# Twelve of sixteen token tiles turned by DMA in 16-bit halves, not by TensorE

## The chip, the cores and the metric

The kernel runs on one core of a Trainium2 chip. A core has a matrix engine (PE, TensorE) and three engines for elementwise work: DVE (VectorE), ACT (ScalarE) and POOL (GpSimd). SP (SyncE) does no arithmetic here; it issues DMAs, and the 16 DMA engines of the core carry them out. Every engine runs its own list of instructions in order and waits on semaphores for the others. The metric is the device time of one execution in microseconds (us), the median over runs. A measurement of this kernel can tell about 0.5%, 4.3 us, from no change.

## The reference

The input x is 2048 tokens of 512 values. It is normalized once, and two blocks read the normalized tokens: a linear attention with a learned feature map, and a mixture of eight experts of which each token takes two.

```python
# x [1, 2048, 512]; 32 heads of 16; 8 experts, hidden width 1792
xn = (x - mean(x)) / sqrt(var(x) + 1e-5)
# A: linear attention
q, k, v = split(xn @ wqkv)                        # heads of 16
pq, pk  = q @ w_phi, k @ w_phi                    # per head
phi_q   = concat(softmax(pq), softmax(-pq))       # per head, 32 wide
phi_k   = concat(softmax(pk), softmax(-pk))
kv, z   = phi_k^T @ v, sum_s phi_k                # per head, over all tokens
A       = concat_heads(phi_q @ kv / (phi_q . z + 1e-6)) @ wo
# B: experts
g       = softmax(xn @ wg); top two, renormalized
B       = sum over the two: g_e * gelu(xn @ w1[e]) @ w2[e]
out     = x + A + B
```

## The kernel before

The tokens come in 16 tiles of 128 (a tile: 128 partitions, one token each, 512 values of 4 bytes), in four chunks of four. The names below are the functions of the kernel, with lines of the kernel before.

**What happens to a tile.** `load_x` brings it in. `stats` (L302, L303, DVE), `rstds` (L306 on ACT, L307 on DVE) and `norm` (L313, DVE) normalize it into a slot of SBUF, and `norm` also has SP store it to DRAM, to `xn_rows` (L315), from where tokens are gathered by expert later. The matrix products need the tile turned, with the 512 features on the partitions. `turn` does that: four transpositions of 128x128 on PE (L326) into one bank of PSUM (two banks for tiles 0 to 3). `transp` then makes two copies from there: ACT casts the turned tile to the matrix format into `xTh` (L341, two instructions of 256 columns), and DVE writes what the cast lost into `xTl` (L342, two subtractions that wait for those casts). High and low parts of data and weights are multiplied in three products (L174 to L176; L474 to L476 in `proj_q`).

**What is done with it.** `proj_k(t)` makes the transformed keys of tile t and its gate logits; ACT takes them out of PSUM (L429, L430). The softmax of the keys works on pairs of tiles: `k_sub` (DVE, L439 to L442), `k_exp` (ACT, L449, behind a table load), `k_norm` (DVE, L454 to L456). `proj_v(t)` makes the values (ACT takes them out, L361), `proj_q` the transformed queries (L479). `kv(p)` (PE, L501) sums the products of keys and values of pair p. After `k_norm(7)` and the last logits the routing begins on DVE (L535 onward): it ranks the tokens with a small product on PE (`route_rank`, L575), and orders the slots of the experts. The experts' layers take the rest of the span.

**What sets the order.** The calls stand in one list, written out by hand; each engine takes its instructions in the order of that list. SP and PE are scheduled by hand as well. So an instruction that waits holds back everything behind it on its engine. Buffers come from two pools of slots, and a slot that is freed is given to a later tile; which one is decided when the program is built.

**Around the change.** The list runs, in the part that matters:

- tiles 4 to 7: `norm(4..7)`, `k_sub(0)`, `proj_v(0)`, `proj_v(1)`, `k_sub(1)`, `proj_v(2)`, `proj_v(3)`, then `transp(4..7)` with the turns, `stats(8..11)`, `proj_v(4)`, `proj_v(5)`, `rstds`, `norm(8..11)`;
- tiles 8 to 11: `k_exp(0, 1)`, `k_sub(2)`, `proj_v(6)`, `k_sub(3)`, loads of x for tiles 12 to 15, `proj_v(7)`, `k_norm(0)`, `proj_k(4)`, `k_exp(2, 3)`, `proj_k(5)`, `k_norm(1)`, `transp(8..11)`;
- tiles 12 to 15: `norm(12..15)`, `k_sub(6)`, `proj_k(8)`, `kv(2)`, `kv(3)`, `proj_k(9..11)`, `proj_q(0, 3)`, `transp(12..15)`, `k_norm(5)`, `k_sub(7)`, `k_exp(6, 7)`, `k_norm(6)`, `proj_k(12..14)`, `kv(4)`, `kv(5)`, `proj_k(15)`, `k_norm(7)`, then the routing.

Of the kernel before, what the change touches and what calls it, by code (L numbers as in the profile page):

```python
# [11 lines left out]
F16 = mybir.dt.float16  # L12
I32 = mybir.dt.int32
AF = mybir.ActivationFunctionType
ALU = mybir.AluOpType
# [24 lines left out]
def kernel(  # L40
# [11 lines left out]
    nc = tc.nc  # L52
    P = 128
    S, D = x.shape[1], x.shape[2]
# [256 lines left out]
    def norm(t):  # L311
        n = slot([P, D], name="xn")
        nc.vector.tensor_scalar(n, xt[t // 2][:, t % 2, :], mv[:, t, 0:1], rstd[:, t:t + 1],  # L313
                                op0=ALU.subtract, op1=ALU.mult)
        nc.sync.dma_start(xs[t * 512:(t + 1) * 512, :].rearrange("(p a) f -> p (a f)", a=4), n)  # L315
        xn[t] = n
        if t % 2:
            free(xt.pop(t // 2))

    turned = {}  # L320

    def turn(t):
        a = bank("pT")
        turned[t] = a, bank("pT") if t < 4 else a
        for k in range(KD):
            nc.tensor.transpose(turned[t][k // 2][:, k * P:(k + 1) * P], xn[t][:, k * P:(k + 1) * P], ident)  # L326
        free(xn.pop(t))

    def transp(t):
        c, j = divmod(t, TPC)  # L330
        if j == 0:
            xTh[c] = [slot([P, 2, 512], F32R, name="xTh", keep=c == 1) for _ in range(2)]
            xTl[c] = [slot([P, 2, 512], F32R, name="xTl", keep=c == 1) for _ in range(2)]
        if t not in turned:
            turn(t)
        ps = turned.pop(t)
        for h in range(2):
# [4 lines left out]
            nc.vector.tensor_sub(dl, src, f32(dh))  # L342
        free(*ps[:2 if t < 4 else 1])

# [102 lines left out]
    def k_exp(*ts):  # L447
        for t in ts:
            nc.scalar.activation(ek[t], ek[t], AF.Exp)  # L449
# [404 lines left out]
    k_sub(0)  # L854
    proj_v(0)
    proj_v(1)
    k_sub(1)
    proj_v(2)
    proj_v(3)
    for t in range(4, 8):  # L860
        transp(t)
    for t in range(8, 12):
        stats(t)
    proj_v(4)
    proj_v(5)
# [4 lines left out]
    k_sub(2)  # L870
    proj_v(6)
    k_sub(3)
    for t in range(12, 16):
        load_x(t)
    proj_v(7)
    k_norm(0)
    proj_k(4)
    k_exp(2, 3)
    proj_k(5)
    k_norm(1)  # L880
    for t in range(8, 12):
        transp(t)
    k_norm(2)
    proj_k(6)
    k_norm(3)
    k_sub(4)
# [10 lines left out]
    for t in range(12, 16):  # L897
        norm(t)
    k_sub(6)
    proj_k(8)  # L900
# [5 lines left out]
    proj_q(0, 3)  # L906
    for t in range(12, 16):
        transp(t)
    k_norm(5)
# [803 lines left out]
```

## Time and profile before

| | |
|---|---|
| time, median of three runs | 858.99 us (858.55 to 862.88) |
| the profiled execution | 858.56 us |
| its span in the trace | 856.8 us |
| PE busy | 851.3 us, 99% of the span |
| DVE busy | 663.9 us, 77% |
| ACT busy | 438.7 us, 51% |
| granted clock of PE | 1.000 |

The span is what the trace covers; the execution's own time is 1.8 us longer. "Busy" of an engine counts its instructions, without register work and without the issuing of DMAs. A busy PE need not be at its peak: matmuls overlap in the records, so a row's duration is longer than its distance to the next row, and this distance is what a stream of them costs. In a timeline a row is: start, duration, engine, line, operation, output<-input, and behind the count in brackets how long the engine had been idle and what ended that.

### The profile page before, as it was taken

The numbers are of one execution on the slowest core, as the hardware profiler recorded it, in microseconds if no ns is written. First come the engines' busy times: TensorE is split into PE (matmuls) and PEld (weight loads), VectorE is DVE, ScalarE is ACT, GpSimd is POOL, SyncE is SP. The second block draws the span as 40 slices with busy tenths as digits, with TensorE's granted clock in tenths as the row PEclk, the third lists the DMA queues.
The fourth block names the chain that finished last, engine by engine and source line by source line (L and its number), as shares of the span: only waits on it lengthen the run. The fifth ranks groups of instructions, "written<-read, shape, count | busy, mean of one in ns | idle before, by whom it ended". The sixth has DMA issues, their size and how long they took to land.

```text
span 856.8 us, 15997 instructions
## 1 busy us (share of the span) xinstructions
PE 851.3 (99%) x5889; PEld 767.9 (90%) x5889; DVE 663.9 (77%) x1098; ACT 438.7 (51%) x721; POOL 184.4 (22%) x251
## 2 busy tenths in 40 slices
PE   9999999999999999999999999999999999999998
PEld 8888888899999999999999999998787888888886
DVE  6889899887783478878887877987798989846952
ACT  4453522743834364566456665465675566434541
POOL 5000002010004112511241142115511522340011
PEclk9999999999999999999999999999999999999999
DMA  8220106573317441843364346533752736539733
GB/s 298 99 99 2 50 8 191 167 231 101 123 50 221 143 133 37 253 133 113 97 200 151 111 138 159 176 110 123 229 178 87 232 115 205 175 135 384 258 115 100
DMA packets 123575, 126.99 MB, mean 148 GB/s; under 512 B 12518, under 2 KB 87782, under 8 KB 123488
## 3 DMA queue, kind: packets, MB, share of 16 engines
q1 hardware_dynamic: 115408, 106.10, 38.6%
q0 software_dynamic: 7264, 19.36, 7.0%
q8 instruction: 48, 0.79, 0.4%
q10 hardware_dynamic: 816, 0.43, 0.2%
q14 instruction: 39, 0.32, 0.1%
HBM read 98.62 MB, written 27.25 MB: 147 GB/s over the span
## 4 chain that ended last, share of the span: by engine, by line
PE 99%; DMA 0%; DVE 0%; issue 0%
PE pH L174 12%; PE pH L175 12%; PE pH L176 12%; PE pY L1296 9%; PE pY L1334 6%; PE pY L1335 6%; PE pY L1340 6%; PE pY L1266 4%; PE pY L1336 2%; PE pY L1337 2%; PE pY L1342 2%; PE pV L174 2%; PE pK L174 2%; PE pQ L474 2%; PE pV L176 2%; PE pO L176 2%
## 5 line engine op out<-in xcount | busy, mean ns | idle before, releaser
L1220 ACT ACTIVATE gl<-pH 128x276 f32<-128x276 f32 (+6 forms) x182 | 78.1, 436 | 252.6 <-PE pH L176 237.4
L1225 DVE TENSOR_TENSOR h<-gl,h 128x480 fp32r<-128x480 f32 (+6 forms) x112 | 77.8, 695 | 96.5 <-ACT h L1222 76.8
L1233 POOL DMA_INDIRECT y_rows<-keptN,pidx x83 | 90.6, 1091 | 253.3 <-ACT gl L1220 210.1
L176 PE MATMUL pH<-keptR,ws 128*128 128x258 f32 (+3 forms) x276 | 82.8, 300 | 0.0
L174 PE MATMUL pH<-keptR,ws 128*128 128x270 f32 (+3 forms) x240 | 72.5, 302 | 0.0
L175 PE MATMUL pH<-keptR,ws 128*128 128x270 f32 (+3 forms) x240 | 72.4, 301 | 0.0
L1222 ACT CAST h<-gl 128x480 fp32r<-128x480 f32 (+6 forms) x112 | 70.1, 626 | 3.6
L175 PE MATMUL pH<-xgl,ws 128*128 128x260 f32 (+3 forms) x204 | 64.6, 317 | 0.0
L174 PE MATMUL pH<-xgh,ws 128*128 128x260 f32 (+3 forms) x204 | 64.6, 317 | 0.0
L1335 PE MATMUL pY<-h,ws 128*128 128x388 f32 (+4 forms) x180 | 62.4, 347 | 0.0
L276 ACT CAST ws<-keptN 128x1024 fp32r<-128x1024 f32 x55 | 57.5, 1046 | 6.9 <-PE pY L1266 6.9
L176 PE MATMUL pH<-xgh,ws 128*128 128x272 f32 (+3 forms) x188 | 59.2, 315 | 0.0
L276 ACT CAST keptR<-keptN 128x1024 fp32r<-128x1024 f32 (+4 forms) x75 | 50.6, 705 | 16.4 <-remote 4.4
L1334 PE MATMUL pY<-h,ws 128*128 128x416 f32 (+4 forms) x168 | 58.5, 348 | 0.0
L1296 PE MATMUL pY<-h,ws 128*128 128x480 f32 x228 | 56.3, 381 | 0.0
L971 POOL DMA_INDIRECT keptN<-xn_rows,tidx x30 | 34.3, 1145 | 97.0 <-DVE vv L675 46.9
L279 DVE TENSOR_TENSOR ws<-keptN,ws 128x1024 fp32r<-128x1024 f32 x36 | 43.6, 1211 | 13.9 <-ACT ws L276 13.6
L176 PEld LDWEIGHTS pH<-keptR,ws 128*128 128x128 f32 x276 | 52.1, 189 | 1.3
L1296 PEld LDWEIGHTS pY<-h,ws 128*128 128x128 f32 x228 | 42.3, 188 | 10.8 <-issue 2.9
L175 PEld LDWEIGHTS pH<-keptR,ws 128*128 128x128 f32 x240 | 45.3, 189 | 2.2
L176 PE MATMUL pH<-xgh,keptR 128*128 128x272 f32 (+3 forms) x148 | 47.1, 318 | 0.0
L174 PEld LDWEIGHTS pH<-keptR,ws 128*128 128x128 f32 x240 | 45.1, 188 | 1.2
(339 smaller groups left out, 2397.1 us busy)
## 6 DMA issues: line engine op xcount, KB each, us to landing
keptN<-in_B_w_dram SPq DMA_DIRECT2D x172, 256.0 KB
wr<-in_B_w_dram SPq DMA_DIRECT2D x52, 256.0 KB
keptN<-y_rows SPq DMA_DIRECT2D x16, 512.0 KB
x_slots<-keptN SPq DMA_DIRECT2D x25, 256.0 KB
keptN<-in_A_x_dram SPq DMA_DIRECT2D x16, 256.0 KB
xn_rows<-keptN SPq DMA_DIRECT2D x16, 256.0 KB
keptN<-x_slots SPq DMA_DIRECT2D x32, 128.0 KB
keptN<-in_A_x_dram SPq DMA_DIRECT2D x8, 512.0 KB
```

The source lines that it names most:

```text
L174: nc.tensor.matmul(ps, lh, rh, start=(i == 0), stop=False)
L175: nc.tensor.matmul(ps, lh, rl, start=False, stop=False)
L176: nc.tensor.matmul(ps, ll, rh, start=False, stop=(i == n - 1))
L276: nc.scalar.copy(dst_h, src)
L1220: step[:] = [nc.scalar.activation(g[:, c:c + m], ps[:, :m], AF.Gelu_apprx_tanh)]
L1222: nc.scalar.copy(h[:, 0:full], g)
L1225: nc.vector.tensor_sub(h[:, xw:], g, f32(h[:, 0:full]))
L1233: i = nc.gpsimd.indirect_dma_start(out=to, out_offset=bass.IndirectOffsetOnAxis(ap=rows, axis=0), in_=y, in_offset=None)
L1296: nc.tensor.matmul(ps[i][:, 0:w], ws[z][:, D + i * P:D + i * P + P], h[:, low * xw:low * xw + w], start=st and k == 0, stop=last and k == ...
L1334: nc.tensor.matmul(ps[i][:, 0:w - P], vh, h[:, P:w], start=st, stop=False, skip_group_check=True)
L1335: nc.tensor.matmul(ps[i][:, 0:m], vl, h[:, P:cap], start=False, stop=False, skip_group_check=True)
L1340: nc.tensor.matmul(ps[i][:, 0:m], v[0][:, i * P:(i + 1) * P], h[:, gw + P:], start=False, stop=sp_, skip_group_check=True)
```

## The change

Tiles 0 to 3 are turned as before. For tiles 4 to 15 the four transpositions on PE are gone, and so is the bank of PSUM. In their place:

- `norm` allocates a slot of twice the size; the normalized tile lies in its first half.
- `to_planes(t)`: ACT copies the tile, read as 1024 half-words of 16 bits for each token, into the second half of the slot, sorted into a plane of the 512 low halves and a plane of the 512 high halves (L327 of the changed kernel). Then SP issues one transposing DMA (L331) that turns the 128x1024 half-words, as eight blocks of 128x128, into a slot `pl` that two tiles share.
- `to_words(t)`: ACT joins the turned planes to words of 32 bits again, into the second half of the tile's slot (L336).
- `transp(t)` reads that half in SBUF where it read PSUM before; its two casts and two subtractions stay (now L361, L362).

Lines of other functions move by up to 40: `proj_v`'s L361 is now L381, L429 is L449, L449 is L469, L479 is L499, L315 is L317.

The list of calls is also written anew around these steps: tiles 4 to 7 are turned between `proj_v(0)` and `proj_v(4)`, one at a time, and `stats(8..11)` stand behind `proj_v(4)` and `transp(7)`; for tiles 8 to 11 the planes are made around `proj_v(6)` and `proj_v(7)`, the loads of x for tiles 12 to 15 stand behind them on SP, and the joining stands behind `proj_k(5)` and `proj_k(6)`; for tiles 12 to 15 the planes are made right behind each `norm`, and the joining stands where `transp` stood.

The tile numbers in the names below are those of slots (`keptN_77`) and of banks (`pK_1014`). Two places show what moved.

**ACT, from the reciprocal deviations of tiles 12 to 15 on.** Before: the eight rows behind `rstd` take the keys of tiles 8 to 11 and their logits out of PSUM, then comes one bank of queries, then the casts of the turned tile 12.

```order
L306 ACTIVATE rstd<-mv,epst 128x4 [waits DVE_49]
L429 COPY keptN_82<-pK_1022 128x32x15 [waits DMAHW1_49,DVE_49,PE_49]
L430 COPY logits<-pK_1022 128x8
L429 COPY keptN_82<-pK_1102 128x32x15 [waits DMAHW2_49,DVE_49,PE_49]
L430 COPY logits<-pK_1102 128x8
L429 COPY keptN_72<-pK_1117 128x32x15 [waits DMAHW3_49,DVE_49,PE_49]
L430 COPY logits<-pK_1117 128x8
L429 COPY keptN_72<-pK_1133 128x32x15 [waits DMAHW4_49,DVE_49,PE_49]
L430 COPY logits<-pK_1133 128x8
L479 COPY keptN_77<-pQ_1148 128x512 [waits PE_49]
L341 CAST xTh_1162<-pT_1166 128x2x128 [waits PE_49]
L341 CAST xTh_1163<-pT_1166 128x2x128 [waits DVE_49]
```

Now: four rows that split tiles 12 to 15 stand ahead of the same eight (of which the first three are shown here).

```order
L307 ACTIVATE rstd<-mv,epst 128x4 [waits DVE_49]
L327 COPY keptN_77<-keptN_77 128x1024 [waits DVE_49]
L327 COPY keptN_73<-keptN_73 128x1024 [waits DVE_49,Pool_49]
L327 COPY keptN_75<-keptN_75 128x1024 [waits DVE_49,PE_49]
L327 COPY keptN_74<-keptN_74 128x1024 [waits DMAHW2_49,DVE_49]
L449 COPY keptN_90<-pK_1014 128x32x15 [waits PE_49]
L450 COPY logits<-pK_1014 128x8
L449 COPY keptN_90<-pK_1094 128x32x15 [waits PE_49]
```

Behind the rest of the eight comes, for each tile, a row that joins it, which waits for the transposing DMA, and the two casts:

```order
L499 COPY keptN_80<-pQ_1140 128x512 [waits PE_49]
L336 COPY keptN_77<-keptN_84 128x2x512 [waits DMAHW6_49,Activation_49]
L361 CAST xTh_1155<-keptN_77 128x2x128 [waits Activation_49]
L361 CAST xTh_1156<-keptN_77 128x2x128
L336 COPY keptN_73<-keptN_84 128x2x512 [waits DMAHW0_49]
L361 CAST xTh_1155<-keptN_73 128x2x128 [waits Activation_49]
```

So the first cast of tile 12 now stands behind five more rows of ACT, four splits and a join, and each later tile's casts behind one more.

**SP, from the stores of tiles 4 to 7 on.** Before, the eight stores of tiles 4 to 11 stand together:

```order
L315 DMA xn_rows<-keptN_84 128x512 [waits DMAHW1_49,DVE_49]
L315 DMA xn_rows<-keptN_82 128x512 [waits DMAHW2_49,DVE_49]
L315 DMA xn_rows<-keptN_72 128x512 [waits DMAHW3_49,DVE_49]
L315 DMA xn_rows<-keptN_74 128x512 [waits DMAHW4_49,DVE_49]
L315 DMA xn_rows<-keptN_81 128x512 [waits DMAHW5_49,DVE_49]
L315 DMA xn_rows<-keptN_77 128x512 [waits DMAHW6_49,DVE_49]
```

Now the four transpositions of tiles 4 to 7 stand behind their stores, each waiting for the split of its tile on ACT, and the stores of tiles 8 to 11 behind those:

```order
L317 DMA xn_rows<-keptN_84 128x512 [waits DMAHW1_49,DVE_49]
L317 DMA xn_rows<-keptN_82 128x512 [waits DMAHW2_49,DVE_49]
L317 DMA xn_rows<-keptN_72 128x512 [waits DMAHW3_49,DVE_49]
L317 DMA xn_rows<-keptN_74 128x512 [waits DMAHW4_49,DVE_49]
L331 DMA_TRANSPOSE keptN_76<-keptN_84 128x8x128 [waits DMAHW5_49,PE_49,Activation_49]
L331 DMA_TRANSPOSE keptN_76<-keptN_82 128x8x128 [waits DMAHW6_49,PE_49,Activation_49]
L331 DMA_TRANSPOSE keptN_77<-keptN_72 128x8x128 [waits DMAHW7_49,Activation_49]
L331 DMA_TRANSPOSE keptN_77<-keptN_74 128x8x128 [waits DMAHW0_49,Activation_49]
L317 DMA xn_rows<-keptN_78 128x512 [waits DMAHW1_49,DVE_49]
```

The stores have not moved against each other; the transpositions are between them.

The diff:

```diff
--- before.py
+++ after.py
@@ -11,6 +11,7 @@
 F32R = mybir.dt.float32r
 F16 = mybir.dt.float16
 I32 = mybir.dt.int32
+U16 = mybir.dt.uint16
 AF = mybir.ActivationFunctionType
 ALU = mybir.AluOpType
 AX = mybir.AxisListType
@@ -309,21 +310,40 @@
     xn = {}
 
     def norm(t):
-        n = slot([P, D], name="xn")
+        both = slot([P, 2, D], name="xn")
+        n = both[:, 0, :]
         nc.vector.tensor_scalar(n, xt[t // 2][:, t % 2, :], mv[:, t, 0:1], rstd[:, t:t + 1],
                                 op0=ALU.subtract, op1=ALU.mult)
         nc.sync.dma_start(xs[t * 512:(t + 1) * 512, :].rearrange("(p a) f -> p (a f)", a=4), n)
-        xn[t] = n
+        xn[t] = both
         if t % 2:
             free(xt.pop(t // 2))
 
+    planes = {}
+
+    def to_planes(t):
+
+        a = xn[t].bitcast(U16)
+        nc.scalar.copy(a[:, 1, :].rearrange("p (h c) -> p h c", h=2),
+                       a[:, 0, :].rearrange("p (c h) -> p h c", h=2))
+        if t % 2 == 0:
+            planes[t // 2] = slot([P, 2, D], name="pl")
+        nc.sync.dma_start_transpose(
+            planes[t // 2].bitcast(U16)[:, t % 2, :].rearrange("p (b n) -> p b n", n=P), a[:, 1, :])
+
+    def to_words(t):
+
+        nc.scalar.copy(xn[t].bitcast(U16)[:, 1, :].rearrange("p (x h) -> p h x", h=2),
+                       planes[t // 2].bitcast(U16)[:, t % 2, :].rearrange("p (h x) -> p h x", h=2))
+        if t % 2:
+            free(planes.pop(t // 2))
+
     turned = {}
 
     def turn(t):
-        a = bank("pT")
-        turned[t] = a, bank("pT") if t < 4 else a
+        turned[t] = bank("pT"), bank("pT")
         for k in range(KD):
-            nc.tensor.transpose(turned[t][k // 2][:, k * P:(k + 1) * P], xn[t][:, k * P:(k + 1) * P], ident)
+            nc.tensor.transpose(turned[t][k // 2][:, k * P:(k + 1) * P], xn[t][:, 0, k * P:(k + 1) * P], ident)
         free(xn.pop(t))
 
     def transp(t):
@@ -331,16 +351,16 @@
         if j == 0:
             xTh[c] = [slot([P, 2, 512], F32R, name="xTh", keep=c == 1) for _ in range(2)]
             xTl[c] = [slot([P, 2, 512], F32R, name="xTl", keep=c == 1) for _ in range(2)]
-        if t not in turned:
+        if t < 4 and t not in turned:
             turn(t)
-        ps = turned.pop(t)
+        ps = turned.pop(t) if t < 4 else [xn[t][:, 1, :]] * 2
         for h in range(2):
             dh = xTh[c][h][:, :, j * P:(j + 1) * P]
             dl = xTl[c][h][:, :, j * P:(j + 1) * P]
             src = ps[h][:, h * 256:(h + 1) * 256].rearrange("p (k n) -> p k n", k=2)
             nc.scalar.copy(dh, src)
             nc.vector.tensor_sub(dl, src, f32(dh))
-        free(*ps[:2 if t < 4 else 1])
+        free(*(ps if t < 4 else [xn.pop(t)]))
 
 
     vt = {}
@@ -853,15 +873,25 @@
         norm(t)
     k_sub(0)
     proj_v(0)
+    to_planes(4)
+    to_planes(5)
     proj_v(1)
     k_sub(1)
+    to_planes(6)
+    to_words(4)
+    transp(4)
     proj_v(2)
+    to_planes(7)
+    to_words(5)
+    transp(5)
     proj_v(3)
-    for t in range(4, 8):
-        transp(t)
+    to_words(6)
+    transp(6)
+    proj_v(4)
+    to_words(7)
+    transp(7)
     for t in range(8, 12):
         stats(t)
-    proj_v(4)
     proj_v(5)
     rstds(8, TPC)
     for t in range(8, 12):
@@ -869,19 +899,27 @@
     k_exp(0, 1)
     k_sub(2)
     proj_v(6)
+    to_planes(8)
+    to_planes(9)
     k_sub(3)
+    proj_v(7)
+    to_planes(10)
+    to_planes(11)
     for t in range(12, 16):
         load_x(t)
-    proj_v(7)
     k_norm(0)
     proj_k(4)
     k_exp(2, 3)
+    k_norm(1)
     proj_k(5)
-    k_norm(1)
-    for t in range(8, 12):
+    for t in (8, 9):
+        to_words(t)
         transp(t)
     k_norm(2)
     proj_k(6)
+    for t in (10, 11):
+        to_words(t)
+        transp(t)
     k_norm(3)
     k_sub(4)
     proj_k(7)
@@ -896,6 +934,7 @@
     ln_stats(12)
     for t in range(12, 16):
         norm(t)
+        to_planes(t)
     k_sub(6)
     proj_k(8)
     kv(2)
@@ -905,6 +944,7 @@
     proj_k(11)
     proj_q(0, 3)
     for t in range(12, 16):
+        to_words(t)
         transp(t)
     k_norm(5)
     k_sub(7)
```

## The prediction

> **What bounds the kernel now.** I read the page first: the busy times, then the chain of waits that ended last.
>
> ```profile
> span 856.8 us, 15997 instructions
> PE 851.3 (99%) x5889; PEld 767.9 (90%) x5889; DVE 663.9 (77%) x1098; ACT 438.7 (51%) x721; POOL 184.4 (22%) x251
> PE 99%; DMA 0%; DVE 0%; issue 0%
> ```
>
> PE is busy all the time and is 99% of the chain, so work taken from PE looks like time saved. The change takes 48 transpositions from it. What a group of 16 costs is its distance to the next row, in the PE timeline:
>
> ```profile
> 90.00 1.91 PE L326 MATMUL pT<-ident,keptN 128*128 128x128 f32 x16
> 91.66 0.47 PE L174 MATMUL pK<-wfh,xTh 128*128 128x496 f32 x1
> ```
>
> 1.66 us, and the first product behind it lasts 0.47 us where its neighbours last 0.39, so about 1.74. There are three such groups: 5.2 us is the most that the change can bring, 0.6%.
>
> Next I asked who else is full in the stage where the tiles are turned. Busy times in two stretches of 20 us (PE, PEld, DVE, ACT, POOL, granted clock, DMA share, GB/s):
>
> ```profile
> 80.00:100.00 20.00, 20.00 (x113) 16.71 (x115) 16.01 (x32) 8.98 (x21) 0.97 (x3) 1.00 0.14 53
> 100.00:120.00 20.00, 20.00 (x334) 16.44 (x330) 18.08 (x58) 6.22 (x15) 0.00 (x0) 1.00 0.01 3
> ```
>
> DVE has 18 of 20 us behind 100 us. Its timeline and PE's show that the two finish side by side:
>
> ```profile
> 95.88 1.21 DVE L454 TENSOR_REDUCE sk<-keptN 128x64 f32<-128x1024 f32 x1
> 106.05 1.22 DVE L456 TENSOR_TENSOR keptN<-keptN,sk 128x1024 f32<-128x1024 f32 x1
> 113.30 1.00 DVE L563 TENSOR_TENSOR cum<-cum 128x128 f16<-128x128 f16 x4
> ...
> 99.88 1.27 PE L501 MATMUL kv<-keptN,keptN 128*18 128x32 f32 x128
> 106.69 1.46 PE L501 MATMUL kv<-keptN,keptN 128*18 128x32 f32 x128
> 114.33 0.23 PE L575 MATMUL pR<-m,tri 128*128 128x128 f16 x1
> ```
>
> The last `k_norm` ends at 107.27; the group of `kv` that needs it (pairs 6 and 7) takes 1.46 us where the one at 99.88 takes 1.27, so it already waits there. `cum` ends at 114.30 and PE ranks at 114.33. From 95.88 to 107.27 DVE has no row with an idle time. So PE cannot be earlier there unless DVE is: **the saved 5.2 us become waiting, and what DVE does at 95.88 decides.** What sets that is the turning of tiles 12 to 15, where DVE waits for ACT's casts.
>
> **The change, part by part.** Prices: a copy of 128x1024 on ACT has a near row in the page; those of ACT around tiles 12 to 15 are in its timeline.
>
> ```profile
> L276 ACT CAST ws<-keptN 128x1024 fp32r<-128x1024 f32 x55 | 57.5, 1046 | 6.9 <-PE pY L1266 6.9
> 85.82 0.56 ACT L429 COPY keptN<-pK 128x480 f32<-128x480 f32 x1 [0.87 <-DVE keptN L313]
> 86.33 0.58 ACT L429 COPY keptN<-pK 128x480 f32<-128x480 f32 x1
> 90.19 0.59 ACT L479 COPY keptN<-pQ 128x512 f32<-128x512 f32 x1 [2.12 <-PE pQ L476]
> 90.67 0.38 ACT L341 CAST xTh<-pT 128x256 fp32r<-128x256 f32 x1
> 91.54 0.65 ACT L341 CAST xTh<-pT 128x256 fp32r<-128x256 f32 x2 [0.49 <-DVE xTl L342]
> ```
>
> A split or a join handles 1024 half-words in each partition: 1.05 us if the count of elements decides, as in the first row, and 0.55 if their bytes do. I take 1.05, since the row has the same count; on ACT the next instruction starts about 0.1 before the end of the one before (90.19 + 0.59 against 90.67), so 0.94 in a row of them. The planes are read with a stride of two half-words, which no row shows; at worst that doubles a copy, 2.1 us.
>
> The transposing DMA has no row. Its bounds come from the nearest transfers:
>
> ```profile
> q1 hardware_dynamic: 115408, 106.10, 38.6%
> 35.00:37.00 2.00, 2.00 (x10) 1.68 (x9) 2.00 (x5) 0.60 (x1) 0.00 (x0) 1.00 1.05 402
> 33.82 1.79 SPq L315 DMA_DIRECT2D xn_rows<-keptN  x4
> 149.28 0.53 SPq L979 DMA_DIRECT2D x_slots<-keptN  x1
> 151.70 0.69 DVE L441 TENSOR_TENSOR keptN<-keptN,mk 128x512 f32<-128x512 f32 x1 [0.82 <-DMA x_slots<-keptN]
> ```
>
> Four stores run at 402 GB/s, so 256 KB take 0.65 us of the queues: the lower bound. The queue q1 spends 0.386 x 16 x 856.8 us on 115,408 packets, 46 ns each, of 919 bytes on average. The transposition has 1024 rows of 256 bytes, 64 for each of the 16 engines: 0.8 us if time goes by bytes, 2.9 if each row costs a packet. I take 1.4, nearer the bytes since the store moves as much. From issue to use a store takes 2.4 us (149.28 to 151.70). The Trainium skill is at odds with itself here. "Advanced Engine Details and Errata" (X-Bar Transpose (TRN2)) has transposing DMAs nearly as fast as plain ones, 350 to 400 GB/s, about 0.7 us for a tile. "VectorE: DVE Perf Modes" (The three transpose paths) gives 1309 ns for one block of 128x128, against 390 ns on TensorE, and advises TensorE where PSUM will do; eight blocks one after the other would be 10.5 us. No run has shown either yet.
>
> *Tiles 4 to 7.* DVE before:
>
> ```profile
> 39.26 0.69 DVE L442 TENSOR_TENSOR keptN<-mk,keptN 128x512 f32<-128x512 f32 x1
> 41.54 0.43 DVE L342 TENSOR_TENSOR keptR<-pT,keptR 128x256 fp32r<-128x256 f32 x1 [1.60 <-ACT keptR L341]
> 46.33 0.68 DVE L302 BATCH_NORM_STATS2 st<-keptN 128x6 f32<-128x512 f32 x1
> 62.83 0.42 DVE L342 TENSOR_TENSOR xTl<-pT,xTh 128x256 fp32r<-128x256 f32 x1
> 67.62 1.21 DVE L454 TENSOR_REDUCE sk<-keptN 128x64 f32<-128x1024 f32 x1
> ```
>
> The fourth store is issued about 35.1 and has moved by 37.5. The first transposition follows it (+1.4, and 0.4 to be seen): 39.3. SP issues four of them, at 0.45 each by the stores' row, beside that. Then ACT sets the pace, with a join (0.94), two casts (0.27 each), the eviction of a value bank (0.48), 2.0 a tile, and the split of tile 7 (0.94) once: 39.3 + 8.9 + 0.4 for the last subtraction, 48.5. The statistics of tile 8 began at 46.33: **+2.1**.
>
> *Tiles 8 to 11.* The eight subtractions stand from 62.83 to 67.62, 4.8 us, as each second one waits for a cast behind the bank that it shares. Now nothing is shared, ACT has time ahead (the joins stand behind `proj_k(5)`), and eight in a row cost 2.8: **-2.0**. So DVE is at `norm(12)` as before, 85.3 for 85.19.
>
> *Tiles 12 to 15.* Here the splits go ahead of everything on ACT.
>
> ```profile
> 85.19 1.92 DVE L313 TENSOR_SCALAR keptN<-keptN,mv,rstd 128x512 f32<-128x512 f32 x4
> 88.81 0.69 DVE L442 TENSOR_TENSOR keptN<-mk,keptN 128x512 f32<-128x512 f32 x1
> 91.08 0.42 DVE L342 TENSOR_TENSOR xTl<-pT,xTh 128x256 fp32r<-128x256 f32 x1 [1.59 <-ACT xTh L341]
> 91.95 0.76 DVE L342 TENSOR_TENSOR xTl<-pT,xTh 128x256 fp32r<-128x256 f32 x2 [0.44 <-ACT xTh L341]
> 93.15 0.76 DVE L342 TENSOR_TENSOR xTl<-pT,xTh 128x256 fp32r<-128x256 f32 x2 [0.44 <-ACT xTh L341]
> 95.54 0.42 DVE L342 TENSOR_TENSOR xTl<-pT,xTh 128x256 fp32r<-128x256 f32 x1 [0.44 <-ACT xTh L341]
> ```
>
> The first norm ends near 85.8; four splits to 89.65; the four evictions of keys queued behind them at 0.51 (85.82 to 86.33) and that of the queries (0.48) to 92.2; join and cast to 93.65. The four transpositions land beside that, the last near 92. Before, the first subtraction stood at 91.08. A tile then takes ACT 1.62 (a join of 1.05, which its first cast waits for, and the casts), where it took 1.20 (91.95 to 93.15): the last subtraction ends at 93.65 + 3 x 1.62 + 0.7 = 99.2, and `k_norm(5)` starts there instead of 95.88: **+3.3**. DVE has no idle time up to 107.27 to take it up, so `kv(7)`, the ranking and the start of the experts move by 3.3.
>
> PE in this stage: with two groups of transpositions gone it is through `proj_q(0, 3)` at 90.00 - 3.5 = 86.5 and then waits for tile 12 until 93.65, 7 us with no work. What that does to its clock no row in mid-kernel shows; the start does:
>
> ```profile
> 3.79 1.94 PE L378 MATMUL pF<-ident,keptN 128*128 128x128 f32 x8 [0.19 <-DMA keptN<-in_A_wqkv_dram]
> 8.62 1.04 PE L378 MATMUL pF<-ident,keptN 128*128 128x128 f32 x8
> ```
>
> The same eight transpositions take 1.94 us after the idle start and 1.04 five us later: half the rate for some 6 us. Half rate for 3.4 to 6.8 us (up to as long as it was idle) costs 1.7 to 3.4 us of products. PE then has 15 us to `kv(7)` (91.66 to 106.69) and reaches it at 110.4 to 112.1; DVE at 107.27 + 3.3 = 110.6. So 0 to 1.5 of it shows; I take **+0.6**. A rule of the Trainium skill speaks against the change here ("TensorE: Matmul & The Clock Gate", Part 1: the HAM clock gate): an idle window of about 3.4 us halves the clock, and it comes back after as long a busy one. By it the loss is 1.7 us, the lower end, and the sum would come to +3.3; the start agrees with the halving.
>
> Costed at nothing: the twelve DMAs' traffic (share 0.14 and 0.01 in the stretches above, so it has room) and SP's queue (the loads of x behind `proj_v(7)` are needed at 81 us only). If that cover went, `stats(12)` would be late next.
>
> **Sum:** the first two stages cancel to +0.1, which the +3.3 of the third holds already (it starts from 85.3). Against the profiled execution of 858.56: 858.56 + 3.3 + 0.6 = **862.5**. The median is 858.99, 0.43 above the execution the sum starts from.
>
> **Rivals.**
>
> *The transposition is slow.* Up to about 1.9 us it hides behind ACT's pace of 2.0 a tile; beyond, the joins wait for it, and behind a waiting join on ACT stand the evictions of values and keys and so PE; all twelve then run one behind another ahead of work that waits, and each further us costs 12. At 2.9 (a packet for each row): 858.6 + 12 = 870.5; at 3.5, 878. For: rows of 256 bytes, a quarter of the mean packet. Against: by bytes it is 0.8, well under the threshold. A slow 16-bit copy does the same with less: of the 24 copies about 14 are on the path, so 1.3 us instead of 1.05 gives +3.5 more, 866. If the page with 1309 ns per block is right (eight in series), 12 x 8.6 = 103 us would come on top, 962; that outcome lies inside this rival's chance.
>
> *The clock stays low longer*, as at the start and beyond `kv(7)`: 15 us at half rate cost 7.5, of which 1.9 are covered: +3.3 + 3.0 to 5.6, 865 to 867.
>
> *Copies go by bytes*, 0.55 us: stage 12 to 15 gains 8 x 0.5 = 4.0 against +3.3, tiles 4 to 7 lose nothing: DVE is 2 to 2.7 us earlier and PE follows: 856. Against: the row of 1046 ns.
>
> *DVE's delay is taken up*, somewhere in the routing by waits on DMAs: 859. Against: the tie at 114.33, and 99% of the chain on PE.
>
> **How the numbers follow.** Forecast, 860.5 to 865: 0.50; slow transposition or copies, 866 to 880 and beyond: 0.25; long low clock: 0.10; copies by bytes, 854 to 858: 0.08; taken up: 0.07. The likeliest gives 862.5. The bounds of the unknown prices (0.65 to 2.9 us) give +2.5 to +12, so the range is 859.5 to 872; about 0.1 is left on each side. A measurement tells 0.5%, 4.3 us, from no change: faster is below 854.7, half of the copies' case and a little, 0.05; slower is above 863.3: the slow cases (0.25 + 0.10) and a quarter to a third of the forecast, 0.49; within, 0.46.
>
> **What would show it.** In the changed profile: ACT rows of 128x1024 at 1.05 us; the first transposition seen by ACT near 39.3; DVE's `stats(8)` at 48.5, `norm(12)` at 85.3, `k_norm(5)` at 99.2; a wait of PE of about 7 us ahead of `proj_k(12)`, with 128x496 rows of 0.4 turning to 0.6 and more behind it; `kv(7)` ending near 111.5. Wrong it is if the joins wait long for DMAs (the first rival), or if `k_norm(5)` is at 96 or earlier (the third).

## The result, and the profile after

The change makes the kernel slower: 870.62 us (868.61 to 871.54, four runs) against 860.08 (858.55 to 862.88, four runs), a ratio of 1.0116 with a 95% interval of 1.0081 to 1.015. A second set of runs on another occasion gave 867.54 against 858.06, 1.011 (1.0094 to 1.0125). The profiled execution took 871.54 us, its span is 869.4.

The page of the changed kernel, its head, the chain of waits and the hardware DMA queue:

```profile
span 869.4 us, 15942 instructions
PE 851.6 (98%) x5841; PEld 764.6 (88%) x5841; DVE 663.7 (76%) x1098; ACT 464.3 (53%) x745; POOL 183.4 (21%) x251
PE 90%; ACT 5%; DVE 3%; DMA 1%; issue 1%; SPq 0%; ACTq 0%; DVEq 0%
q1 hardware_dynamic: 128080, 109.24, 40.0%
```

PE was 99% of the chain, now it is 90%. ACT has 25.6 us more work and holds 5% of the chain, DVE 3%. PE lost 48 transpositions, 5.2 us by the prediction's rows, and is busy for as long as before (in the second traces of both kernels 849.2 and 850.6 us). About 2.7 us of what it got back are the clock, as the stretches show (columns as before, the clock ahead of the last two):

```profile
80.00:100.00 20.00, 11.44 (x46) 9.15 (x45) 13.33 (x27) 13.95 (x24) 0.42 (x2) 0.81 0.41 105
100.00:120.00 20.00, 20.00 (x328) 16.42 (x327) 16.83 (x32) 10.02 (x20) 0.22 (x1) 0.93 0.01 3
```

From 80 to 100 us PE works 11.44 of 20 us, at a granted clock of 0.81. Its timeline there, and at the two places where PE and DVE had been level before:

```profile
96.89 0.78 PE L175 MATMUL pK<-wfh,xTh 128*128 128x496 f32 x1 [8.56 <-ACT xTh L361]
97.47 0.61 PE L176 MATMUL pK<-wfl,xTh 128*128 128x496 f32 x1
97.88 0.61 PE L177 MATMUL pK<-wfh,xTl 128*128 128x496 f32 x1
...
103.22 0.39 PE L176 MATMUL pK<-wfl,xTh 128*128 128x496 f32 x1
...
114.66 1.32 PE L521 MATMUL kv<-keptN,keptN 128*18 128x32 f32 x128
122.17 0.23 PE L595 MATMUL pR<-m,tri 128*128 128x128 f16 x1
```

PE waits 8.56 us for ACT's cast of tile 12, then its products stand 0.41 us apart where they stood 0.22 apart, until about 102.7. The ranking is at 122.17 instead of 114.33. DVE, at the statistics of tile 8, the norms of tile 12, the first and the last subtraction of tiles 12 to 15, and `k_norm(5)` and `k_norm(7)`:

```profile
49.92 0.69 DVE L303 BATCH_NORM_STATS2 st<-keptN 128x6 f32<-128x512 f32 x1
...
68.29 0.76 DVE L362 TENSOR_TENSOR xTl<-keptN,xTh 128x256 fp32r<-128x256 f32 x2 [1.18 <-ACT xTh L361]
...
88.12 1.92 DVE L315 TENSOR_SCALAR keptN<-keptN,mv,rstd 128x512 f32<-128x512 f32 x4
...
96.87 0.76 DVE L362 TENSOR_TENSOR xTl<-keptN,xTh 128x256 fp32r<-128x256 f32 x2 [4.45 <-ACT xTh L361]
98.86 0.76 DVE L362 TENSOR_TENSOR xTl<-keptN,xTh 128x256 fp32r<-128x256 f32 x2 [1.22 <-ACT xTh L361]
...
102.84 0.76 DVE L362 TENSOR_TENSOR xTl<-keptN,xTh 128x256 fp32r<-128x256 f32 x2 [1.23 <-ACT xTh L361]
103.51 1.22 DVE L474 TENSOR_REDUCE sk<-keptN 128x64 f32<-128x1024 f32 x1
...
113.70 1.22 DVE L476 TENSOR_TENSOR keptN<-keptN,sk 128x1024 f32<-128x1024 f32 x1
```

`k_norm(5)` starts at 103.51, 7.6 us later than before (95.88), and `k_norm(7)` ends at 114.92 instead of 107.27: the same 7.65. So both engines come to `kv(7)` late by nearly the same. What makes DVE wait is ACT (its groups from 30 to 110 us of the span, then its timeline):

```profile
L336 ACT COPY keptN<-keptN 128x1024 uint16<-128x1024 uint16 x12 | 16.3, 1360 | 1.8 <-DMA keptN<-keptN 1.8
L327 ACT COPY keptN<-keptN 128x1024 uint16<-128x1024 uint16 x12 | 12.0, 1045 | 1.2 <-DVE keptN L315 1.2
L361 ACT CAST xTh<-keptN 128x256 fp32r<-128x256 f32 x16 | 5.7, 405 | 0.3
```

```profile
39.02 1.36 ACT L336 COPY keptN<-keptN 128x1024 uint16<-128x1024 uint16 x1 [1.79 <-DMA keptN<-keptN]
...
88.70 3.89 ACT L327 COPY keptN<-keptN 128x1024 uint16<-128x1024 uint16 x4 [0.83 <-DVE keptN L315]
92.49 0.55 ACT L449 COPY keptN<-pK 128x480 f32<-128x480 f32 x1
...
95.00 1.40 ACT L336 COPY keptN<-keptN 128x1024 uint16<-128x1024 uint16 x1
96.44 0.71 ACT L361 CAST xTh<-keptN 128x256 fp32r<-128x256 f32 x2
97.05 1.34 ACT L336 COPY keptN<-keptN 128x1024 uint16<-128x1024 uint16 x1
```

A split takes 1.045 us, a join 1.36. Twelve joins waited for a transposition only once, 1.79 us at 39.02. In the last stage ACT goes without a pause from the first split at 88.70 to the last cast, and each tile costs it 1.99 us.

**How the runs are compared below.** The start of `norm(4)` on DVE lay at 32.4 to 33.8 us in the twelve further traces and the two above, whatever the kernel. The rest from the ranking to the end of the span was 742.2 to 744.9 us in all of them but the first trace of the change, where it was 747.2. This scatter is as large as some of what is asked for. So three places are given in us after the start of `norm(4)`: the start of `norm(12)`, the end of `k_norm(7)`, the start of the ranking; they repeat within 0.3 us. (`k_sub`, `k_exp`, `k_norm` and `kv` work on one tile each; where the description of the kernel says pair, it should say tile.) One execution of the kernel before, in the set with the median of 858.00 below, took 1709.06 us, and the ratios leave it out. Before: 51.94, 74.02, 81.08. The change: 54.91, 81.71, 88.96.

### The profile page after: what moved, and what is told of

Same layout as the page of the kernel before. It is cut to its first block, busy times and chain, and to the rows that moved or that the text cites. A ratio compares the mean times of both kernels' runs of the same rounds, so it can differ in the third digit from the quotient of the medians.

```text
span 869.4 us, 15942 instructions
## 1 busy us (share of the span) xinstructions
PE 851.6 (98%) x5841; PEld 764.6 (88%) x5841; DVE 663.7 (76%) x1098; ACT 464.3 (53%) x745; POOL 183.4 (21%) x251
## 4 chain that ended last, share of the span: by engine, by line
PE 90%; ACT 5%; DVE 3%; DMA 1%; issue 1%; SPq 0%; ACTq 0%; DVEq 0%
PE pH L175 12%; PE pH L176 12%; PE pH L177 12%; PE pY L1336 8%; PE pY L1374 6%; PE pY L1375 6%; PE pY L1380 6%; PE pY L1306 4%; PE pY L1376 2%; PE pY L1377 2%; PE pY L1382 2%; PE pO L177 1%; PE pO L175 1%; PE pO L176 1%; ACT keptN L336 1%; PE pQ L494 1%
## 5 line engine op out<-in xcount | busy, mean ns | idle before, releaser
L1336 PEld LDWEIGHTS pY<-h,ws 128*128 128x128 f32 x228 | 42.3, 188 | 10.5 <-issue 2.5
```

The source lines that it names most:

```text
L1336: nc.tensor.matmul(ps[i][:, 0:w], ws[z][:, D + i * P:D + i * P + P], h[:, low * xw:low * xw + w], start=st and k == 0, stop=last and k == ...
```

## The experiments

| kernel | norm(12) | k_norm(7) ends | ranking | PE's wait for tile 12 | median us, against before beside it | ratio |
|---|---|---|---|---|---|---|
| before | 51.94 | 74.02 | 81.08 | none | | |
| before, second trace | 51.95 | 74.04 | 81.11 | none | 859.56, one run | |
| the change | 54.91 | 81.71 | 88.96 | 8.56 | 870.62 / 860.08 | 1.0116 (1.0081 to 1.015) |
| the change, second trace | 54.86 | 81.66 | 89.20 | 8.56 | 867.54 / 858.06 | 1.011 (1.0094 to 1.0125) |
| 12 to 15 by PE | 54.91 | 75.30 | 82.38 | 0.98 | 861.34 / 860.77 | 1.0005 (0.9992 to 1.0019) |
| only 8 to 11 by DMA | 51.25 | 72.17 | 79.23 | none | 858.56 / 860.77 | 0.997 (0.9955 to 0.9985) |
| only 12 to 15 by DMA | 51.95 | 78.76 | 85.81 | 3.74 | 862.57 / 858.00 | 1.006 (1.0042 to 1.0078) |
| idle products in the wait | 54.90 | 81.72 | 88.79 | 0.67 | 866.04 / 860.77 | 1.0073 (1.0046 to 1.01) |
| DVE filled | 54.91 | 78.36 | 88.21 | 8.55 | 866.80 / 860.77 | 1.009 (1.0054 to 1.0126) |
| both of these | 54.81 | 78.32 | 86.20 | 0.66 | 863.70 / 858.06 | 1.0065 (1.005 to 1.008) |
| all by DMA, reordered | 51.58 | 75.12 | 82.73 | 3.62 | 860.89 / 858.06 | 1.0034 (1.0022 to 1.0046) |
| join in the other order | 53.58 | 79.68 | 86.76 | 7.92 | 865.22 / 858.00 | 1.0093 (1.0075 to 1.0111) |
| 4 to 11 by DMA, statistics between | 51.53 | 71.94 | 79.01 | none | 856.23 / 858.06 | 0.9978 (0.9968 to 0.9987) |
| that, with the join's other order | 50.21 | 71.31 | 78.36 | none | 855.54 / 858.09 | 0.9971 (0.996 to 0.9981) |

My theory was that two chains end side by side at the ranking: DVE behind ACT's copies, and PE behind its wait and the half rate. The rivals were each of the two alone, and the transposing DMAs.

### Each stage by itself

Tiles 12 to 15 turned by PE, 4 to 11 as in the change:

```diff
-        norm(t)
-        to_planes(t)
+        norm(t)            # t = 12..15
...
-        to_words(t)
         transp(t)          # t = 12..15, with turn(t) on PE
```

> Tiles 12 to 15 turned by PE again, tiles 4 to 11 as in the change. My theory (two chains end side by side at the ranking: DVE behind ACT's copies, PE behind its wait and the half rate): the last stage costs nothing any more, and what is left is the delay that norm(12) already has in the change (88.12 against 85.19). DVE's k_norm(7) ends near 110.2 instead of 107.27 and 114.92, the ranking stands near 117.2 (114.33 before, 122.17 in the change), and the time is about 2.9 us above the kernel before. Rival, the low clock alone makes the loss: with no wait of 8 us left the time is that of the kernel before or up to 3 us below it. Rival, the transposing DMAs make the loss: 8 of 12 are left, and so about two thirds of it, 7 us.

The ranking is 1.3 us later than before, where I expected 2.9; the time is that of the kernel before within 0.2%. So 6.6 of the 7.9 us go when the last stage is taken back. Of the 2.97 us by which `norm(12)` is late, 1.7 come back in the last stage, since PE, with two groups of turns less to do, stands ready for tile 12 where DVE had waited 1.59 us before.

Only tiles 8 to 11 by DMA (the order of the kernel before for 4 to 7 and 12 to 15):

> Only tiles 8 to 11 by DMA; tiles 4 to 7 and 12 to 15 turned by PE in the order of the kernel before. My theory: this stage gives DVE 0.6 to 2 us (the subtractions no longer share a bank with the casts) and PE 1.7, so the ranking comes 0.6 to 1.7 us earlier than 114.33 and the time is 0.6 to 1.7 us below the kernel before. Rival, every transposing DMA and its copies cost time wherever they stand: a third of the loss, +2.5 to +3.5 us.

It is 0.3% faster, with an interval that leaves out 1, though the gain is below the 0.5% that a measurement of this kernel can tell by itself: `norm(12)` comes 0.69 us earlier, and the ranking 1.85, a little more than I expected. That two thirds of it appear only in the last stage has the reason just given. Eight of the twelve DMAs were to cost about 7 us by the third rival and four of them about 3; the ranking moved by +1.3 and by -1.85. The third rival falls here.

Only tiles 12 to 15 by DMA:

> Only tiles 12 to 15 by DMA, with the lines of the change in that stage; tiles 4 to 11 turned by PE in the order of the kernel before. Measured by differences in the change, this stage alone makes DVE 4.7 us later, and tiles 4 to 11 only 1.3 in the end (run with tiles 12 to 15 by PE). My theory: norm(12) at 51.9 us after norm(4) as before, PE waits about 4 us for tile 12, k_norm(7) ends near 78.8, the ranking at 85.5 to 86.5, the time about 5 us above the kernel before. Rival, the loss needs the earlier stages (PE ahead by 3.5 us more, a wait of 8.6 us and the low clock): without them the time is that of the kernel before, within 1.5 us.

As expected: `norm(12)` as before, the ranking 4.73 us later, the time 0.6% up. PE waits 3.74 us for tile 12, and still has to wait for DVE at the end:

```profile
111.56 0.72 PE L522 MATMUL kv<-keptN,keptN 128*18 128x32 f32 x64 [0.83 <-DVE keptN L477]
```

The rival, that without the earlier stages there is no loss, falls. But the stages do not simply add: alone, the last one costs 4.7 us and the earlier ones 1.3, 6.0 together, where the change has 7.9. The missing 1.9 us fit the 1.7 that came back above: with tiles 12 to 15 by DMA DVE waits 4.4 us for tile 12 whether `norm(12)` is late or not, so nothing takes its lateness up.

### The two chains

The change with idle products on PE ahead of `proj_k(12)`:

```diff
+    gap = bank("gap")
+    for _ in range(72):
+        nc.tensor.matmul(gap[:, 0:256], idle[:, 0:P], idle, start=True, stop=True)
+    free(gap)
     for t in range(12, 16):
         to_words(t)
```

> The change, with 72 idle products (128x256, 16-bit, zeros) put on PE ahead of proj_k(12), where PE waits 8.56 us. They add nothing to the result. Both theories: the granted clock stays 1.00 and the products of proj_k(12) stand 0.22 us apart instead of 0.41. My theory: PE reaches kv(6) 2.7 us earlier, near 112, but kv(7) still needs k_norm(7) at 114.9, so the ranking stays near 122.0 and the time within 0.5 us of the change. Rival, the low clock sets the end: ranking near 119.5, 2.7 us less than the change.

The clock stays at 1.00 and the products behind tile 12 stand 0.22 us apart. PE comes to `kv(6)` early and waits there for DVE:

```profile
84.00:97.00 13.00, 12.33 (x92) 10.27 (x91) 7.85 (x19) 9.36 (x18) 0.10 (x1) 1.00 0.65 133
...
112.17 0.73 PE L521 MATMUL kv<-keptN,keptN 128*18 128x32 f32 x64
114.30 0.72 PE L521 MATMUL kv<-keptN,keptN 128*18 128x32 f32 x64 [1.40 <-DVE keptN L476]
```

The ranking moves by 0.17 us. The low clock alone does not set the end. In time I had expected at most 0.5 us against the change, and that did not come: the median is 4.6 us below the first set of the change and 1.5 below the second. The ranking accounts for 0.2 to 0.4 of this. The rest lies ahead of `norm(4)` and behind the ranking, stretches that the edit does not touch: they take 775.0 us together here, 775.9 and 780.5 in the two traces of the change. The kernel before, measured beside it, spread from 857.65 to 862.59 us, so these medians do not decide between the theories; the places in the trace do.

The change with DVE's work put where it waits:

```diff
-    for t in range(12, 16):
-        to_words(t)
-        transp(t)
-    k_norm(5)
-    k_sub(7)
+    k_norm(5)
+    for t in (12, 13):
+        to_words(t)
+        transp(t)
+    k_sub(7)
+    for t in (14, 15):
+        to_words(t)
+        transp(t)
```

> The change, with k_norm(5) put ahead of the joins of tiles 12 to 15 and k_sub(7) between those of tiles 13 and 14, so that DVE works where it waited 4.45 and 1.2 us; PE and ACT keep their order. My theory: k_norm(7) ends near 111.6 instead of 114.92, but PE, late by its wait and the half rate, still reaches kv(6) at 114.7, and the ranking stays near 122.1: the time within 0.5 us of the change. Rival, DVE alone sets the end: ranking near 118.9, 3.3 us less than the change.

DVE ends `k_norm(7)` 3.35 us earlier, as expected, and the ranking moves by 0.75. PE is there no sooner, and in the last row below DVE waits 2.08 us for the ranking:

```profile
109.56 1.22 DVE L476 TENSOR_TENSOR keptN<-keptN,sk 128x1024 f32<-128x1024 f32 x1
...
113.11 1.32 PE L521 MATMUL kv<-keptN,keptN 128*18 128x32 f32 x128
120.63 0.23 PE L595 MATMUL pR<-m,tri 128*128 128x128 f16 x1
...
120.99 0.17 DVE L610 SCALAR_TENSOR_TENSOR ek<-pR,rev 128x8 f32<-128x8 f32 x1 [2.08 <-PE pR L599]
```

The 0.75 is PE's own: the half rate lasted for 10 products here, for 14 in the change, after the same wait, and four products at 0.19 us too much make 0.76. (In the second trace of the change it lasted for 12. `kv(6)` starts 0.34 us earlier there, but then `kv(7)` takes 1.21 us instead of 0.72, partly in a gap of 0.30 that the trace puts down to no other engine, and the ranking is late again.) The time is again lower than expected, 0.7 us below the second set of the change and 3.8 below the first, where the ranking gives 0.75 to 1.

Both edits together:

> Both edits of the earlier runs together in the changed kernel: the 72 idle products on PE ahead of proj_k(12), and k_norm(5) and k_sub(7) on DVE between the joins. Alone, the first took 0.2 us from the way to the ranking, the second 0.75. My theory (two chains side by side): together they take 2.7 to 3.3, so the ranking comes 85.7 to 86.3 us after norm(4), where the change has 88.96. Rival, the edits act one by one: 0.2 + 0.75, 88.0. In time: 2.5 to 3.5 us less than the change against about 1.

The ranking comes 2.76 us earlier than in the change, inside the range that the theory gave and three times the sum of the two alone (0.92); the time is 3.8 us below the change measured in the same set, a little more than expected. This is what shows the two chains: each covers for the other, and only where both are shortened does the end move far. The traces show it a second way. `cum`, DVE's last step ahead of the ranking, ends 0.03 us before the ranking with the idle products, so there DVE comes last. In the change it ends 0.2 us before (0.5 in the second trace), with DVE filled 2.4 and with both edits 0.9, so there PE comes last, in the change by little.

The change with every DMA and every copy, in another order:

```diff
+    stats(8)               # ahead of to_planes(6); stats(9), (10), (11) behind transp(4), (5), (6)
...
-    for t in range(8, 12):
-        stats(t)           # behind transp(7)
...
-    proj_k(8)              # and 9 to 11
+    proj_k(8, False)       # without taking the keys out of PSUM
...
+    k_norm(5)
+    to_words(12); transp(12); to_words(13); transp(13)
+    k_sub(7)
+    k_out(8); k_out(9)     # the keys of tiles 8, 9 out of PSUM
+    to_words(14); transp(14); to_words(15); transp(15)
+    k_out(10); k_out(11)
```

> The change with all twelve tiles by DMA and every copy, only in another order: stats(8..11) between the subtractions of tiles 4 to 7 on DVE; k_norm(5) ahead of the joins of tiles 12 to 15 and k_sub(7) between them; the evictions of proj_k(8..11) on ACT behind the joins of tiles 13 and 15. My theory, that the loss is where DVE and PE wait behind ACT and not the transposing DMA or the copies' own time: norm(12) comes 51 to 52 us after norm(4) (54.9 in the change, 51.9 before), PE's wait falls to 4 us or less, the ranking comes near 81 us after norm(4), so the whole loss of 7.9 is gone and the time is that of the kernel before, within 0.3%. Rival, the DMAs or ACT's added 29 us cost what they cost: at most 3.3 us come back, as in the run with both edits.

6.2 of the 7.9 us are gone, so neither the DMAs nor ACT's added 28 us of copies are the loss by themselves; where others wait behind them is. Against the kernel before 1.65 us remain, where I had expected none. DVE shows one place that I had not counted, `k_norm(6)`, which waits for its exponential behind all of ACT's joins and evictions; and PE still waits 3.62 us, and 1 us behind that wait its products stand 0.41 apart again, for 3 us. Here PE comes last: `cum` ends 0.6 us ahead of the ranking.

```profile
101.69 1.22 DVE L482 TENSOR_REDUCE sk<-keptN 128x64 f32<-128x1024 f32 x1 [2.97 <-ACT keptN L477]
...
90.86 0.50 PE L175 MATMUL pK<-wfh,xTh 128*128 128x496 f32 x1 [3.62 <-ACT xTh L361]
91.19 0.38 PE L176 MATMUL pK<-wfl,xTh 128*128 128x496 f32 x1
91.86 0.78 PE L177 MATMUL pK<-wfh,xTl 128*128 128x496 f32 x1 [0.29 <-DVE xTl L362]
92.44 0.62 PE L175 MATMUL pK<-wfh,xTh 128*128 128x496 f32 x1
```

### The price of the join

```diff
-        nc.scalar.copy(xn[t].bitcast(U16)[:, 1, :].rearrange("p (x h) -> p h x", h=2),
-                       planes[...][:, t % 2, :].rearrange("p (h x) -> p h x", h=2))
+        nc.scalar.copy(xn[t].bitcast(U16)[:, 1, :].rearrange("p (x h) -> p x h", h=2),
+                       planes[...][:, t % 2, :].rearrange("p (h x) -> p x h", h=2))
```

> The change, with the join's elements taken in another order: it writes the words one after another, both halves of each, and reads from the two planes in turn, where it now writes all low halves and then all high halves, every second half-word. The result is the same. The joins took 1.36 us where I had said 1.05, the splits 1.05. My theory: twelve joins 0.31 too long, eight of them in the stages of tiles 4 to 7 and 12 to 15 and two in that between, are the 4.4 us by which DVE is later than I forecast (7.7 against 3.3). If writing every second half-word is what makes them long, they take 1.05 now, k_norm(7) ends near 78 us after norm(4) (81.7 in the change) and the ranking stands at 85 to 86. Rival, the two-plane access makes them long: they take 1.36 or more, and nothing moves.

```profile
L336 ACT COPY keptN<-keptN 128x1024 uint16<-128x1024 uint16 x12 | 14.1, 1178 | 1.8 <-DMA keptN<-keptN 1.8
```

The joins take 1.18 us: the order of the elements is part of their price, but not all of what is above 1.05. `k_norm(7)` ends 2.03 us earlier, which is 11 times the 0.18 us by which a join became shorter. So about 11 of the 12 joins lie on DVE's way, and by that proportion 0.31 too much in each of them makes an estimated 3.4 us. The ranking came 2.2 us earlier; joins of 1.05 were to bring 3 to 4. The expected 1.05 and the rival's 1.36 both missed: the edit changes the writing and the reading side at once, so what each of them costs in the new order is not shown.

### Again, for the scatter

> The changed kernel itself once more, for a second trace and for times beside the kernel before on one chip. In the first trace the ranking on PE came 88.96 us after norm(4) (81.08 before), +7.9, and the rest of the span was 747.2 us (742.5 before), +4.7; in the four traces of the first experiments that rest was 742.6 to 744.9. My theory: the +7.9 comes again within 0.7 us (the half rate can last shorter), the +4.7 is scatter of the later stages; the time is 7 to 10 us above the kernel before. Rival, the change also costs something behind the ranking: the rest is 747 us again and the time 11 to 13 us above.

> The kernel before itself, for a second trace. The two traces of the change put the ranking at 88.96 and 89.20 us after norm(4), which accounts for 7.9 to 8.1 us; the medians of one chip differ by 9.5. My theory: the kernel before starts norm(4) at 33.25 in its one trace, the other kernels at 32.4 to 33.3, and this scatter of the first stage and that behind the ranking (742.5 here) make the rest: norm(4) at 32.4 to 32.9, the ranking 81.1 after it. Rival, its trace is typical and the change costs 1.5 us in a place not looked at.

The ranking of the change lies at 89.2, and the rest behind it is 743.04 us: the +4.7 of the first trace did not come again, and I count it as scatter. The kernel before repeats to 0.03 us at the ranking, with `norm(4)` at 33.81, later and not earlier as I had expected. The traces explain 7.9 to 8.1 us; the medians of the two sets differ by 10.5 and 9.5. Of the 1.4 to 2.6 us between them 0.3 lie outside the span: an execution of the change took 2.1 to 2.2 us more than its span, one of the kernel before 1.8 to 1.9. The rest I have not found. It may be the scatter ahead of `norm(4)` and behind the ranking, which is as large; a cost of about 1 us in a place not looked at, as the rival has it, is not excluded.

### Versions faster than both

Tiles 4 to 11 by DMA, tiles 12 to 15 by PE, and `stats(8..11)` on DVE between the subtractions of tiles 4 to 7, where it waited 2.67, 1.73 and 1.72 us for the joins:

> Tiles 4 to 11 by DMA, tiles 12 to 15 by PE, and stats(8..11) between the subtractions of tiles 4 to 7, where DVE waits 2.7, 1.7 and 1.7 us for the joins in the change. My theory: norm(12) comes 51 to 52 us after norm(4) (54.9 with the statistics behind), the ranking near 78.5 (81.08 before, 79.23 with tiles 8 to 11 alone), so the time is about 2.5 us below the kernel before and 0.5 to 1 below that with tiles 8 to 11 alone. Rival, DVE's chain in the last stage decides: no better than the run with tiles 4 to 11 by DMA and the old order, 82.4, and the time that of the kernel before.

The same, with the join in its other order:

> The run with tiles 4 to 11 by DMA and the statistics between the subtractions, with the join in the order that took 1.18 us. My theory: eight joins shorter by 0.18, of which those of tiles 4 to 9 have DVE waiting behind them, bring norm(12) from 51.5 to about 50.5 us after norm(4); PE, which has the four turns of tiles 12 to 15 left to do, takes up part of it, so the ranking comes at 78.3 to 78.8 (79.0 with the long join, 81.1 before) and the time is 2 to 3 us below the kernel before. Rival, PE sets that place by now: the ranking stays at 79.0 and the time at 0.2% below the kernel before.

The first is 0.22% faster than the kernel before, with `norm(12)` at 51.53 where it was 54.91 with the statistics behind, and the ranking 2.07 us earlier, at 79.01 where I had expected 78.5. The second is 0.29% faster (855.54 against 858.09), the ranking at 78.36, as expected. The kernel with tiles 8 to 11 alone, measured on another occasion, is as fast within the intervals, and is the smallest edit. All three gains are below the 0.5% that a measurement of this kernel can tell by itself; what supports them is that each interval leaves out 1 and that the ranking, which repeats within 0.3 us, comes 1.9 to 2.7 us earlier.

## Why the prediction was right and where it was wrong

The time lies in the range (859.5 to 872), near its upper end, and not at the likeliest value of 862.5. Against the kernel before the change costs 10.5 and 9.5 us in the two sets, 7.9 to 8.1 up to the ranking, where the forecast was 3.9. It came by a branch that stood among the rivals: the sentence that a slow 16-bit copy at 1.3 us would give 866. That the branch's +3.5 is so near the 3.4 below is partly luck, since it had 14 copies too long by 0.25 and the runs have 11 by 0.31. The range holds the time with little to spare: the prediction's +2.5 to +12 give 861.1 to 870.6, and the 1.5 us that it added on each side have no reason stated. (Its times for the slow transposition, 870.5 to 962, also leave out the +3.9 of its own sum.)

**What bounds the kernel: right.** PE at 99% hid that DVE ends level with it. In every run the ranking follows the later of the two, and 3.5 to 5.2 us taken off PE are worth nothing where DVE is late.

**The price of a split: right** (1.05, measured 1.045). **The price of a join: wrong**, and this is the step that failed. I put split and join under one row, 128x1024 at 1046 ns, with a remark on the stride of the reading side, which cost nothing, and none on that of the writing side. The join took 1.36. With eleven joins on DVE's way that is an estimated 3.4 of the 4.4 us by which DVE was later than forecast (7.7 against 3.3). For the other 1.0 the rows offer two things, neither tested: for tiles 4 to 7 I took 0.94 for a join, as if its cast could start before it ended, but the casts started 1.38 to 1.39 us behind the start of joins of 1.35 to 1.36; and a cast took 405 ns from SBUF where 377 from PSUM was the row. By stages, in us of delay:

| stage | forecast | measured | |
|---|---|---|---|
| tiles 4 to 7 (start of `norm(8)`) | +2.1 | +3.56 | four joins in a row, 2.48 a tile instead of 2.0 |
| tiles 8 to 11 (from there to `norm(12)`) | -2.0 | -0.59 | the join of tile 9 was not done in time, DVE waits 1.18 |
| tiles 12 to 15 (from there to `k_norm(7)`) | +3.2 | +4.72 | 0.4 later at the first subtraction, then 1.99 a tile instead of 1.62 |

The middle stage is where I had assumed cover ("ACT has time ahead") and not worked it out.

**The transposing DMA: right.** The queue's rows before and after give it: 40.0% of 16 engines over 869.4 us, less 38.6% over 856.8, is 273 us of engine time, 17 us of the queue, 1.42 for each of twelve; I had taken 1.4. (It is a rough figure: the same difference gives 1.3 to 2.1 in the runs with four or eight transpositions.) The first one was seen by ACT at 39.02, forecast 39.3. The page of the Trainium skill with 350 to 400 GB/s ("Advanced Engine Details and Errata", X-Bar Transpose (TRN2)) gives an estimate of half of that, 0.7; that with 1309 ns for a block ("VectorE: DVE Perf Modes", The three transpose paths) gives an estimate seven times as large, 10.5, if eight blocks go one after the other. What I had too low is SP's time to issue one, 0.45 by the row of the stores and 1.24 alone as the last section shows; it stayed hidden.

**The clock: the mechanism right, the size hidden.** PE waited 8.56 us, not 7, and its products at half the rate cost it about 2.7 us, inside the 1.7 to 3.4. Of the 0.6 that I added, 0.17 shows, by the run with idle products, since DVE is as late. The rule of the Trainium skill ("TensorE: Matmul & The Clock Gate", Part 1: the HAM clock gate), an idle window of about 3.4 us, agrees with waits of 3.62 and 3.74 us that were followed by half rate and waits of 0.66 to 0.98 that were not. The 1.7 us of loss that I had worked out from it were too few: the half rate lasted 5.8 us behind the wait, not 3.4. The last section says why that length differs from run to run.

**The rivals.** The slow transposition did not come, the slow copy did, in one of its two kinds. The long low clock did not: 14 products, 5.8 us. Copies that go by bytes: no. A delay that is taken up later: no, from the ranking on all traces but the first of the change take 742.2 to 744.9 us, and that one takes longer.

## What to carry to other kernels

Work taken from an engine that is busy 99% of the time gains only as far as the others can keep ahead of it: look for the row where a second engine has no idle time either, and price the change on that engine first. Where two chains end level, an experiment on one of them moves little (0.17 and 0.75 us here) and tells little; shorten both (2.76). An operation that replaces another on a chain should be priced by its access pattern in each direction, and put where somebody else does not queue behind it: twelve splits, joins and DMAs cost 7.9 us in one order and 1.65 in another, and four or eight of them, in the stages that had room, were a gain of about 2.

## What the runs showed of the hardware that I had not expected

- A copy of 1024 half-words on ACT took 1.045 us where it read every second half-word and wrote in a row, 1.36 where it wrote every second half-word, and 1.18 where it wrote in a row and read from two planes in turn. So the side on which the stride lies matters, and so does the order of the elements.
- SP needs 1.24 us to issue a transposition of 128x1024 half-words, and 8.12 us for the first four, which had to wait for ACT's splits as well; a plain store of 256 KB took 0.32 to 0.52. SP's queue in the change:

```profile
35.69 8.12 SPq L331 DMA_TRANSPOSE keptN<-keptN  x4
...
88.69 0.33 SPq L317 DMA_DIRECT2D xn_rows<-keptN  x1
89.77 1.24 SPq L331 DMA_TRANSPOSE keptN<-keptN  x1
95.46 0.52 SPq L317 DMA_DIRECT2D xn_rows<-keptN  x1
```

- After a wait of 3.62 us PE's first product still came at the full rate, and by the clock the half rate began 0.6 us later, for 3.4 us; after 8.56 us it lasted for 10, 12 and 14 products in three traces. The granted clock explains both. In the change it was:

```profile
92.00:93.00 1.00, 0.00 (x0) 0.00 (x0) 0.42 (x1) 1.00 (x3) 0.00 (x0) 0.72 0.78 271
...
102.00:103.00 1.00, 1.00 (x5) 0.83 (x4) 0.16 (x1) 0.97 (x3) 0.00 (x0) 0.66 0.00 0
```

Between these two stretches it was 0.50. So it was halved from about 92.44 to 102.68, for 10.24 us. The same working gives 10.24 us in the second trace and with DVE filled (waits of 8.56 and 8.55), 6.8 with the join's other order (7.92), and 3.4 after the waits of 3.62 and 3.74: three, two and one times 3.4. It fell 2.6, 3.5, 4.1 and 5.0 us after the four long waits had begun. So in these traces the clock changes in steps of 3.4 us whose start is not tied to the wait, and the number of slow products is what is left of the last step when the wait ends.
